# Sigmoid attention and a bilinear feed-forward: x through memory in blocks of 512 tokens, twelve float32 pairs, another spread of the weight decoding

## The chip, the core and the metric

The kernel runs on one core of a Trainium2 chip. The metric is the device time of one execution in microseconds (us); lower is better. Before the change it was 1091.12 us, the median of three runs (1089.79 to 1091.72). One more execution was taken with the hardware profiler on; all views of the profile below are of that execution.

## The reference

```python
# q, k, v: (8 batches, 12 heads, 448 tokens, 64); w1, w2: 768 x 1024; w3: 1024 x 1024; w_out: 1024 x 768
scores = q @ k.T / sqrt(64) - log(448)
attn   = sigmoid(scores) @ v
x      = attn, heads side by side          # 3584 tokens x 768
a, b   = x @ w1, x @ w2
out    = ((a * b) @ w3) @ w_out            # float32
```

The four weights come as float64 (seen as int64 words), so each has to be decoded to float32 on the chip.

## The kernel before, in words

A *pair* is two heads of one batch: 6 pairs in a batch, 48 in all. A pair takes four *slots*, one for each piece of its keys, in the order 0, short (the last 64 keys), 1, 2. A slot puts on TensorE: the scores of the slot, then up to 12 *filler* matmuls, then the attention times v of the slot before (the short piece is held back by one slot more). ScalarE turns scores into sigmoids.

The first `PLAIN` = 9 pairs use float32 matmuls straight on the loaded q, k, v. From then on each operand is split into a high and a low fp32r part, which costs work on VectorE and GpSimd (`split_pair`, `split_v`), two sigmoids for a piece and the subtraction `al` on VectorE. After a pair, `combine` splits its result into `xh` and `xl`, one of the six 128-row pieces (kc) of x for that batch, and keeps it on chip: six tiles of each in `px0` or `px1`, by the parity of the batch.

The filler is `up`: the first products x @ w1 and x @ w2, whose product g is written to memory (`g_dram`). It handles one batch of 448 tokens: 8 chunks of d_ff (fc) times 2 weights times 6 pieces times 3 matmuls, 288 in all, just 12 for each of the 24 slots of a batch. It runs one batch behind attention, so the batch-0 pairs have no filler and the last batch's products come after all attention. A copy of the first accumulator (`a_sb`, ScalarE) and the multiplication (`g`, VectorE) close each fc.

Weights are decoded by "jobs" (`decode_weights`). Jobs 0 to 15 bring w1 and w2, each with one load of 768 KB (`raw`), one ScalarE instruction (`f`), six on VectorE, and then the split into `w` (ScalarE copy, VectorE subtraction). They stand in the first nine pairs, the first eight 3 slots apart, the rest 4/3 slots apart. Jobs 16 to 31 decode w3, half a chunk each, in the second slot of every other pair from pair 12 on, and write it back to memory (`w3_dram`). Each of these loads its raw words right after the job before it has been decoded, two pairs ahead.

After attention: the last batch's `up` beside the decoding of w_out, then w3 @ w_out (w34), then out = g @ w34 in blocks of 512 tokens (`TB`).

The order on TensorE and on SyncE (SP, which issues every DMA) is the order in which the code is written; in the first eight pairs that holds for ScalarE and GpSimd too. VectorE's order, and later ScalarE's and GpSimd's, is chosen by a scheduler at build time. Every engine then works through its list in order, and an instruction that waits holds up all that stand behind it. This holds for SP's DMA issues too.

Of the kernel before, what the change touches and what calls it, by code (L numbers as in the profile page):

```python
# [11 lines left out]
F32 = mybir.dt.float32  # L12
# [13 lines left out]
def sigmoid_attention_bilinear_ffn(  # L26
# [16 lines left out]
    nc = tc.nc  # L43
# [12 lines left out]
    PLAIN = 9  # L56
# [5 lines left out]
    w3_dram = dram.tile([NF, P, NF, P], F32, name="w3_dram")  # L62
    g_dram = dram.tile([NF, P, NT], F32, name="g_dram")

    def split(dst_hi, dst_lo, src, hi_engine, lo_engine):
        hi_engine(out=dst_hi, in_=src)  # L66
        lo_engine.tensor_tensor(out=dst_lo, in0=src, in1=dst_hi, op=ALU.subtract)  # L67

    def load_words(src, pool=None):
        if pool is None:  # L70
            raw = pd.tile([P, NK, P, 2], U32, name="raw", bufs=1)[:, :src.shape[1]]
        else:
            raw = pool.tile([P, *src.shape[1:-1], 2], U32, name="raw")
        nc.sync.dma_start(out=raw, in_=src)
        return raw

    def magnitude(raw):
        f = pd.tile([P, *raw.shape[1:-1]], F32, name="f")
        nc.scalar.activation(f, raw[..., 1].bitcast(F32), AF.Abs, scale=HW_SCALE)  # L79
        return f  # L80
# [26 lines left out]
    px1 = phase_x.enter_context(tc.tile_pool(name="px1", bufs=NK, side="left"))  # L107
    pm = phase_x.enter_context(tc.tile_pool(name="pm", bufs=2, side="left"))
    phase_a = ExitStack()
    px0 = phase_a.enter_context(tc.tile_pool(name="px0", bufs=NK, side="right"))  # L110
    pa = phase_a.enter_context(tc.tile_pool(name="pa", bufs=2, side="right"))
    px = (px0, px1)

    phase_p = ExitStack()
    pp = phase_p.enter_context(tc.tile_pool(name="pp", bufs=3, side="right"))
# [144 lines left out]
    def combine(b, accs):  # L260
        xh = px[b % 2].tile([P, S], F32R, name="xh")
        xl = px[b % 2].tile([P, S], F32R, name="xl")
        if len(accs) == 1:
            split(xh, xl, accs[0][:, :S], nc.scalar.copy, nc.vector)
            return xh, xl
        t = pm.tile([P, S], F32, name="t", bufs=1)
        add_halves(t, [acc[:, :S] for acc in accs])
        split(xh, xl, t, nc.scalar.copy, nc.vector)
        return xh, xl
# [19 lines left out]
    def load_job(i):  # L289
        _, _, cs, src = jobs[i]  # L290
        raws[i] = load_words(src[:, cs], pp) if i < EARLY else load_words(src[:, cs])

    def decode_weights():

        for i, (n, at, cs, _) in enumerate(jobs):
            if i + 2 < EARLY:
                load_job(i + 2)
            for k in (i, i + 1):
                if k not in fs and k in raws:
                    fs[k] = magnitude(raws[k])  # L300
            f = decode(raws.pop(i), fs.pop(i))
            if i + 1 >= EARLY and i + 1 < len(jobs):
                load_job(i + 1)
            if n == 3:
                nc.sync.dma_start(out=w3_dram[at, :, cs], in_=f)
                yield
                continue
            yield
            split(wh[n][:, at, cs], wl[n][:, at, cs], f, nc.scalar.copy, nc.vector)
            yield  # L310

    def up(b, xs, banks):

        for fc in range(NF):
            for n in (1, 2):
                acc = ps.tile([P, 512], F32, name="up", tag=next(banks), bufs=2)
                for kc in range(NK):
                    xh, xl = xs[kc]
                    for m, (w, x) in enumerate(((wh[n], xh), (wh[n], xl), (wl[n], xh))):
                        nc.tensor.matmul(  # L320
                            acc[:, :S], w[:, fc, kc], x,
                            start=(kc == 0 and m == 0), stop=(kc == NK - 1 and m == 2),
                        )
                        if (kc, m) != (NK - 1, 2):
                            yield
                if n == 1:
                    a_sb = pm.tile([P, S], F32, name="a_sb", bufs=1)
                    nc.scalar.copy(out=a_sb, in_=acc[:, :S])
                    yield
            g = pm.tile([P, S], F32, name="g", bufs=1)  # L330
            nc.vector.tensor_tensor(out=g, in0=acc[:, :S], in1=a_sb, op=ALU.mult)
            nc.sync.dma_start(out=g_dram[fc, :, b * S:(b + 1) * S], in_=g)
            yield
# [11 lines left out]
    first = NPAIR * NC  # L345
    starts = [1 + 3 * i for i in range(8)] + [first + 1 + 4 * i // 3 for i in range(8)]
    assert len(starts) == 2 * NF
    later = [(2 * NPAIR + 2 * i) * NC + 1 for i in range(2 * NF)]
    steps = starts + [s + 2 - s // first for s in starts] + later

    EARLY = sum(s < (PLAIN - 1) * NC for s in starts)
# [7 lines left out]
    weights = decode_weights()  # L359
    xs = {b: [] for b in range(B)}  # L360
# [5 lines left out]
    def attend_due(slot):  # L366
        while waiting and waiting[0][0] <= slot:
            _, p, c, ops = waiting.pop(0)
            if c == 0:
                accs[p] = [  # L370
                    ps.tile([P, 512], F32, name="av", bufs=2) for _ in range(1 if p < PLAIN else 2)
                ]
            attend(c, ops, vs[p], accs[p])
            if c == NC - 2:
                b = pairs[p][0]
                xs[b].append(combine(b, accs.pop(p)))
                del vs[p]
# [22 lines left out]
    for p, (b, hp) in enumerate(pairs):  # L400
        if p == PLAIN - 1:
            order.close()
            order.enter_context(tc.manual_schedule(engines={ET.PE, ET.SP}))
        plain = p < PLAIN
        if p == PLAIN - 1:
            phase_p.close()
            pf.append(phase_a.enter_context(tc.tile_pool(name="pf", bufs=2, side="right")))
        qs, kh, kl, ks = splits.pop(p)
        for i, c in enumerate(chunks):
            prepare(p, i)  # L410
# [12 lines left out]
            attend_due(slot)  # L423
            slot += 1
    attend_due(slot)
    take(filler, 10 ** 6)
    take(weights, 10 ** 6)
# [18 lines left out]
    filler = up(B - 1, xs[B - 1], banks)  # L446
# [16 lines left out]
    TB = 512  # L463
# [19 lines left out]
    assert NT % TB == 0  # L483
# [65 lines left out]
```

## Time and profile before

| what | us |
|---|---|
| median of three runs | 1091.12 |
| the profiled execution, whole | 1088.86 |
| its span | 1087.0 |
| TensorE (PE) busy | 1067.2 |
| VectorE (DVE) busy | 720.1 |
| ScalarE (ACT) busy | 563.6 |
| GpSimd (POOL) busy | 194.6 |

In the profile PE is the matmul, PEld the weight load, DVE VectorE, ACT ScalarE, POOL GpSimd, SP or SPq the queue that issues DMAs. L320 is line 320 of the kernel. A row such as `up<-xh,w 128*128 128x448` names the result, the operands and their shapes. "Idle before" names what an engine waited for.

### The profile page before, as it was taken

The numbers are of one execution on the slowest core, as the hardware profiler recorded it, in microseconds if no ns is written. First come the engines' busy times: TensorE is split into PE (matmuls) and PEld (weight loads), VectorE is DVE, ScalarE is ACT, GpSimd is POOL, SyncE is SP. The second block draws the span as 40 slices with busy tenths as digits, with TensorE's granted clock in tenths as the row PEclk, the third lists the DMA queues.
The fourth block names the chain that finished last, engine by engine and source line by source line (L and its number), as shares of the span: only waits on it lengthen the run. The fifth ranks groups of instructions, "written<-read, shape, count | busy, mean of one in ns | idle before, by whom it ended". The sixth has DMA issues, their size and how long they took to land.

```text
span 1087.0 us, 14111 instructions
## 1 busy us (share of the span) xinstructions
PE 1067.2 (98%) x5076; PEld 911.4 (84%) x5076; DVE 720.1 (66%) x1073; ACT 563.6 (52%) x789; POOL 194.6 (18%) x277
## 2 busy tenths in 40 slices
PE   7899899999999999999999999999999999999998
PEld 1246788999999999999999999999999988888886
DVE  6898878888788878887888877749862133123321
ACT  6763567677677776777677766753342011001100
POOL 0002233323323233223323333200000000000000
PEclk9999899999999999999999999999999999999999
DMA  8654444354425336344434534225461032233211
GB/s 265 194 170 126 114 110 130 106 142 124 134 78 161 99 108 162 95 133 116 126 106 128 136 88 106 61 68 183 134 241 51 20 126 77 98 126 126 88 49 48
DMA packets 100693, 129.15 MB, mean 119 GB/s; under 512 B 8016, under 2 KB 82960, under 8 KB 100624
## 3 DMA queue, kind: packets, MB, share of 16 engines
q1 hardware_dynamic: 100624, 128.25, 40.3%
q8 instruction: 40, 0.66, 0.3%
q14 instruction: 29, 0.24, 0.1%
HBM read 98.34 MB, written 29.88 MB: 118 GB/s over the span
## 4 chain that ended last, share of the span: by engine, by line
PE 86%; DVE 9%; DMA 2%; issue 1%; ACT 1%; SPq 1%; DVEq 0%; ACTq 0%
PE up L320 39%; PE up L510 21%; PE av L255 10%; PE sp L199 8%; PE up L494 6%; DVE f L94 1%; PE sp L225 1%; DVE raw L99 1%; DVE w L67 1%; ACT f L79 1%; DVE raw L86 1%; DVE raw L98 1%; DVE f L91 1%; DVE f L102 1%; DVE al L217 0%
## 5 line engine op out<-in xcount | busy, mean ns | idle before, releaser
L320 PE MATMUL up<-xh,w 128*128 128x448 f32 x1536 | 468.2, 368 | 0.0
L320 PEld LDWEIGHTS up<-xh,w 128*128 128x128 f32 x1536 | 289.1, 188 | 32.5 <-issue 6.0
L320 PE MATMUL up<-xl,w 128*128 128x448 f32 x768 | 281.8, 367 | 0.0
L510 PE MATMUL up<-w 128*128 128x512 f32 x1008 | 228.7, 389 | 0.0
L510 PEld LDWEIGHTS up<-w 128*128 128x128 f32 x1008 | 189.2, 188 | 39.3
L180 ACT ACTIVATE ah<-sp,bias 128x896 fp32r<-128x896 f32 x117 | 117.6, 1005 | 110.0 <-PE sp L199 109.4
L67 POOL TENSOR_TENSOR kl<-kk,kh 128x896 fp32r<-128x896 f32 x39 | 87.3, 2238 | 407.6 <-DVE kh L66 407.6
L320 PEld LDWEIGHTS up<-xl,w 128*128 128x128 f32 x768 | 144.6, 188 | 12.9
L217 DVE TENSOR_TENSOR al<-sp,ah 128x896 fp32r<-128x896 f32 x117 | 127.4, 1089 | 42.0 <-ACT sp L180 40.8
L520 DVE COPY o_sb<-up 128x512 f32<-128x512 f32 x42 | 29.0, 691 | 161.0 <-PE up L510 161.0
L66 ACT CAST w<-graw 128x1024 fp32r<-128x1024 f32 x28 | 29.3, 1054 | 175.0 <-PE up L510 170.5
L180 ACT ACTIVATE sp<-sp,bias 128x896 f32<-128x896 f32 x117 | 113.7, 971 | 0.0
L255 PE MATMUL av<-ah,vs 128*128 128x448 f32 x312 | 102.6, 369 | 3.0 <-DVE xl L67 1.4
L67 POOL TENSOR_TENSOR vs<-vv,vs 128x256 fp32r<-128x256 f32 x78 | 71.3, 925 | 100.1 <-DVE vs L66 79.4
L255 PE MATMUL av<-al,vs 128*128 128x448 f32 x234 | 86.3, 369 | 1.5 <-DVE al L217 1.5
L199 PE MATMUL sp<-qs,kh 128*128 128x448 f32 x234 | 86.3, 369 | 0.0
L199 PE MATMUL sp<-qs,kl 128*128 128x448 f32 x234 | 86.2, 369 | 0.0
L239 DVE TENSOR_TENSOR ah<-st,ah 64x448 fp32r<-64x448 f32 x78 | 60.2, 772 | 21.2 <-ACT st L180 19.4
L255 PEld LDWEIGHTS av<-ah,vs 128*128 128x128 f32 x312 | 58.7, 188 | 10.7 <-issue 5.4
L79 ACT ACTIVATE f<-raw 128x768 f32<-128x768 f32 (+2 forms) x48 | 34.1, 710 | 59.9 <-DVE w L67 22.4
L186 ACT COPY t<-av 64x448 f32<-64x448 f32 x78 | 41.2, 529 | 32.4 <-PE av L255 31.3
L180 ACT ACTIVATE ah<-st,bias 64x448 fp32r<-64x448 f32 x78 | 52.2, 669 | 4.1 <-DVE st L187 2.1
(54 smaller groups left out, 1244.7 us busy)
## 6 DMA issues: line engine op xcount, KB each, us to landing
qq<-qT SPq DMA_DIRECT2D x78, 224.0 KB, 3.9
kk<-kT SPq DMA_DIRECT2D x78, 224.0 KB, 4.3
g_dram<-g SPq DMA_DIRECT2D x64, 224.0 KB, 2.0
graw<-g_dram SPq DMA_DIRECT2D x14, 1024.0 KB, 5.3
raw<-w SPq DMA_DIRECT2D x16, 768.0 KB, 5.8
out<-o_sb SPq DMA_DIRECT2D x42, 256.0 KB, 2.0
vv<-vL SPq DMA_DIRECT2D x48, 192.0 KB, 2.7
raw<-w3T SPq DMA_DIRECT2D x16, 512.0 KB, 4.3
```

Source lines behind the costliest of these rows:

```text
L66: hi_engine(out=dst_hi, in_=src)
L67: lo_engine.tensor_tensor(out=dst_lo, in0=src, in1=dst_hi, op=ALU.subtract)
L79: nc.scalar.activation(f, raw[..., 1].bitcast(F32), AF.Abs, scale=HW_SCALE)
L180: nc.scalar.activation(dst, src, AF.Sigmoid, bias=bias[:n], scale=scale)
L186: nc.scalar.copy(out=dst[rows], in_=src[j][others])
L199: nc.tensor.matmul(sp[:, j], k[:, j, at:at + n], qs[:, j], start=m == 0, stop=m == 1)
L217: nc.vector.tensor_tensor(out=al, in0=sp, in1=ah, op=ALU.subtract)
L239: nc.vector.tensor_tensor(out=a[others, j], in0=t[rows], in1=a[rows, j], op=ALU.subtract)
L255: nc.tensor.matmul(accs[j][:, :S], v[:, c, j].rearrange("p u d -> p (u d)"), a[:, j], start=first and m == 0, stop=last and m == len(ops) - 1,
L320: nc.tensor.matmul(acc[:, :S], w[:, fc, kc], x, start=(kc == 0 and m == 0), stop=(kc == NK - 1 and m == 2),)
L494: nc.tensor.matmul(acc[:, :NM], a[:, jc], w[:, jc, ms], start=(jc == 0 and m == 0), stop=(jc == NF - 1 and m == 2),)
L510: nc.tensor.matmul(acc[:, :TB], w[:, fc, ms], g[:, at, fc % NH], start=(fc == 0 and m == 0), stop=(fc == NF - 1 and m == 2),)
```

## The change

1. **x through memory.** After a pair, `combine` now splits into one tile with both parts, and a store (`store_due`) brings it to `x_dram` one slot later (two in the float32 pairs). Only block 0 (tokens 0 to 511: batch 0 and 64 tokens of batch 1) is written straight into its tiles. `load_block` reads blocks 1 to 6 back, 512 KB for each of six pieces. There are eight such tiles: two pieces of the next block are loaded ahead, when fc 6 of the block in work begins; the other four each take the tile of a piece of the block in work, when its last matmul is done.
2. **up in blocks of 512 tokens**, 7 instead of 8, again 288 matmuls each, two batches behind attention: block c starts in the last slot of the first pair of batch c + 2.
3. **PLAIN = 12**: all of batches 0 and 1 is done in float32, without filler beside it.
4. **Jobs 0 to 15** are spread over the first 45 slots, 2.7 slots apart, with the split three slots later; `f` has three buffers instead of two, `raw` four instead of three.
5. **Jobs 16 to 31** stand where they stood, but load their own raw words there: load, decoding and write-back of a job are now written in one slot.

```diff
-    PLAIN = 9
+    TB = 512
+    PLAIN = 2 * NPAIR
+    x_dram = dram.tile([NK, P, 2, NT], F32, name="x_dram")
...
-    def magnitude(raw):
-        f = pd.tile([P, *raw.shape[1:-1]], F32, name="f")
+    def magnitude(raw, pool=pd):
+        f = pool.tile([P, *raw.shape[1:-1]], F32, name="f", bufs=3 if pool is not pd else 2)
...
-    px1 = phase_x.enter_context(tc.tile_pool(name="px1", bufs=NK, side="left"))
+    px = phase_x.enter_context(tc.tile_pool(name="px", bufs=NK + 2, side="left"))
...
-    pp = phase_p.enter_context(tc.tile_pool(name="pp", bufs=3, side="right"))
+    pp = phase_p.enter_context(tc.tile_pool(name="pp", bufs=4, side="right"))
...
+    def combine(b, kc, accs, due):
...
+        at = b * S
+        n = min(max(TB - at, 0), S)
+        if n:
+            if b == 0:
+                blocks[0][kc] = px.tile([P, 2, TB], F32R, name="x")
+            x = blocks[0][kc][:, :, at:at + n]
+            split(x[:, 0], x[:, 1], src[:, :n], nc.scalar.copy, nc.vector)
+        if n < S:
+            x = pa.tile([P, 2, S], F32R, name="xs")[:, :, n:]
+            split(x[:, 0], x[:, 1], src[:, n:], nc.scalar.copy, nc.vector)
+            stores.append((due, x_dram[kc, :, :, at + n:at + S], x))
+
+    def load_block(c, kc):
+        blocks[c][kc] = px.tile([P, 2, TB], F32R, name="x")
+        nc.sync.dma_start(
+            out=blocks[c][kc].bitcast(F32), in_=x_dram[kc, :, :, c * TB:(c + 1) * TB]
+        )
...
-            f = decode(raws.pop(i), fs.pop(i))
-            if i + 1 >= EARLY and i + 1 < len(jobs):
-                load_job(i + 1)
-            if n == 3:
-                nc.sync.dma_start(out=w3_dram[at, :, cs], in_=f)
+    def decode_job(i):
+        if i + 3 < EARLY:
+            load_job(i + 3)
+        elif i >= EARLY:
+            load_job(i)
+        for k in (i, i + 1):
+            if k in raws and k not in fs:
+                fs[k] = magnitude(raws[k], pp if k < EARLY else pd)
+        f = decode(raws.pop(i), fs[i])
+        n, at, cs, _ = jobs[i]
+        if n == 3:
+            nc.sync.dma_start(out=w3_dram[at, :, cs], in_=f)
...
-    def up(b, xs, banks):
+    def up(c, banks):
+
+        xs, following = blocks[c], c + 1 if c + 1 in blocks else None
         for fc in range(NF):
+            if fc == NF - 2 and following:
+                for kc in range(2):
+                    load_block(following, kc)
             for n in (1, 2):
...
+                    if (fc, n) == (NF - 1, 2) and following and kc + 2 < NK:
+                        load_block(following, kc + 2)
...
-    starts = [1 + 3 * i for i in range(8)] + [first + 1 + 4 * i // 3 for i in range(8)]
...
+    EARLY = 2 * NF
+    starts = [1 + 27 * i // 10 for i in range(EARLY)]
+    steps = {s + 3: [(split_job, i)] for i, s in enumerate(starts)}
+    for i, s in enumerate(starts + [(2 * NPAIR + 2 * i) * NC + 1 for i in range(2 * NF)]):
+        steps.setdefault(s, []).append((decode_job, i))
...
+            store_due(slot)
             prepare(p, i)
...
-            take(weights, steps.count(slot))
-            if b > 0 and (hp, i) == (0, 2):
+            for step, n in steps.get(slot, ()):
+                step(n)
+            if b > 1 and (hp, i) == (0, NC - 1):
                 take(filler, 10 ** 6)
-                filler = up(b - 1, xs[b - 1], itertools.repeat("up"))
+                filler = up(b - 2, itertools.repeat("up"))
```

Two places where the order of instructions moves. The first is SP's list around a w3 job. Before the change, for one job in mid-attention (g is the store of a product, vv, qq and kk the inputs of the pairs ahead, `raw<-w3T` the words of a job, `w3_dram<-f` a decoded job written back):

```order
L332 DMA g_dram_67<-g_1925 128x448
L144 DMA vv_1953<-vL 128x3x128
L148 DMA vv_1953<-vL 64x128 x2
L74 DMA raw_1973<-w3T 128x4x256
L305 DMA w3_dram_66<-f_1965 128x512
L135 DMA qq_1995<-qT 64x2x448 x2
L135 DMA kk_1996<-kT 64x2x448 x2
L332 DMA g_dram_67<-g_2059 128x448
```

After the change, for the first pair of batch 3 (pair 18), where block 0 of `up` ends and block 1 begins (`x_dram<-xs` is the store of pair 17's x, `x<-x_dram` the load of a piece of block 1):

```order
L359 DMA g_dram_68<-g_1689 128x512
L286 DMA x_dram_67<-xs_1730 256x1x448
L145 DMA vv_1746<-vL 128x3x128
L149 DMA vv_1746<-vL 64x128 x2
L77 DMA raw_1758<-w3T 128x4x256
L327 DMA w3_dram_66<-f_1760 128x512
L290 DMA x_1781<-x_dram_67 128x2x512
L136 DMA qq_1792<-qT 64x2x448 x2
L136 DMA kk_1793<-kT 64x2x448 x2
L290 DMA x_1814<-x_dram_67 128x2x512
L290 DMA x_1819<-x_dram_67 128x2x512
L290 DMA x_1824<-x_dram_67 128x2x512
```

Before, `raw_1973` belongs to the next job and `f_1965` comes from words that were loaded two pairs earlier; now `f_1760` comes from `raw_1758`, the load just ahead of it in the list, and the last four loads of block 1 stand behind that store. The same rows in the same order stand at pairs 24, 30, 36 and 42: w3 jobs fall on pairs 12, 14, 16, ..., 42, and the blocks change on 18, 24, 30, 36 and 42.

The second is VectorE's list at pair 18 after the change (al of the pair's pieces 1 and 2, the decoding of job 19, then the operands of pair 20 and `al` of pair 19):

```order
L218 TENSOR_TENSOR al_1812<-sp_1798,ah_1809 128x896
L240 TENSOR_TENSOR ah_1803<-st_1753,ah_1803 64x448 x2
L69 CAST vs_1835<-vv_1746 128x4x64 x2
L218 TENSOR_TENSOR al_1848<-sp_1840,ah_1845 128x896
L89 TENSOR_SCALAR raw_1758<-raw_1758 128x512
L94 TENSOR_SCALAR f_1760<-f_1760 128x512
L97 SCALAR_TENSOR_TENSOR f_1760<-f_1760,raw_1758 128x512
L101 TENSOR_SCALAR raw_1758<-f_1760 128x512
L102 SCALAR_TENSOR_TENSOR raw_1758<-raw_1758 128x512
L105 TENSOR_TENSOR f_1760<-f_1760,raw_1758 128x512
L159 CAST qs_1907<-qq_1792 128x896
```

The six instructions of the job now stand together, two slots later than the code names them, between `al` of the fourth slot and the first instruction on the operands of pair 20.

More of the change, by code (lines that the diff above doesn't have):

```diff
@@ L55, in sigmoid_attention_bilinear_ffn @@
     scale = 1.0 / math.sqrt(D)
-    PLAIN = 9
+    TB = 512
+    assert NT % TB == 0 and S <= TB <= 2 * S
+    PLAIN = 2 * NPAIR
     pw = ctx.enter_context(tc.tile_pool(name="pw", bufs=4))
@@ L67, in split, with load_words @@
         lo_engine.tensor_tensor(out=dst_lo, in0=src, in1=dst_hi, op=ALU.subtract)
-    def load_words(src, pool=None):
-        if pool is None:
-            raw = pd.tile([P, NK, P, 2], U32, name="raw", bufs=1)[:, :src.shape[1]]
+    def load_words(src, pool):
+        if pool is pd:
+            raw = pd.tile([P, NF // 2, P, 2], U32, name="raw", bufs=1)
         else:
@@ L258, in attend, with store_due @@
                 )
-    def combine(b, accs):
-        xh = px[b % 2].tile([P, S], F32R, name="xh")
-        xl = px[b % 2].tile([P, S], F32R, name="xl")
+    blocks = {c: {} for c in range(NT // TB)}
+    stores = []
+    def combine(b, kc, accs, due):
         if len(accs) == 1:
[L264 to L269, printed above, removed]
+            src = accs[0][:, :S]
+        else:
+            src = pa.tile([P, S], F32, name="t", bufs=1)
+            add_halves(src, [acc[:, :S] for acc in accs])
+        at = b * S
[9 more added lines that the diff above has]
+            stores.append((due, x_dram[kc, :, :, at + n:at + S], x))
+    def store_due(slot):
+        while stores and stores[0][0] <= slot:
+            _, dst, x = stores.pop(0)
+            nc.sync.dma_start(out=dst, in_=x.bitcast(F32))
+    def load_block(c, kc):
[3 more added lines that the diff above has]
+        )
     wh, wl = {}, {}
@@ L290, in load_job @@
         _, _, cs, src = jobs[i]
[L291 to L300, printed above, removed]
-            f = decode(raws.pop(i), fs.pop(i))
-            if i + 1 >= EARLY and i + 1 < len(jobs):
-                load_job(i + 1)
-            if n == 3:
[L305 to L310, printed above, removed]
@@ L314, in up, with split_job @@
+    def split_job(i):
+        n, at, cs, _ = jobs[i]
+        split(wh[n][:, at, cs], wl[n][:, at, cs], fs.pop(i), nc.scalar.copy, nc.vector)
+    def up(c, banks):
+        xs, following = blocks[c], c + 1 if c + 1 in blocks else None
         for fc in range(NF):
+            if fc == NF - 2 and following:
+                for kc in range(2):
+                    load_block(following, kc)
             for n in (1, 2):
-                acc = ps.tile([P, 512], F32, name="up", tag=next(banks), bufs=2)
+                acc = ps.tile([P, TB], F32, name="up", tag=next(banks), bufs=2)
@@ L325, in up @@
                             yield
+                    if (fc, n) == (NF - 1, 2) and following and kc + 2 < NK:
+                        load_block(following, kc + 2)
                 if n == 1:
-                    a_sb = pm.tile([P, S], F32, name="a_sb", bufs=1)
-                    nc.scalar.copy(out=a_sb, in_=acc[:, :S])
+                    a_sb = pm.tile([P, TB], F32, name="a_sb")
+                    nc.scalar.copy(out=a_sb, in_=acc)
                     yield
-            g = pm.tile([P, S], F32, name="g", bufs=1)
-            nc.vector.tensor_tensor(out=g, in0=acc[:, :S], in1=a_sb, op=ALU.mult)
-            nc.sync.dma_start(out=g_dram[fc, :, b * S:(b + 1) * S], in_=g)
+            g = pm.tile([P, TB], F32, name="g")
+            nc.vector.tensor_tensor(out=g, in0=acc, in1=a_sb, op=ALU.mult)
+            nc.sync.dma_start(out=g_dram[fc, :, c * TB:(c + 1) * TB], in_=g)
             yield
@@ L343, in sigmoid_attention_bilinear_ffn @@
     pairs = [(b, hp) for b in range(B) for hp in range(NPAIR)]
-    first = NPAIR * NC
-    starts = [1 + 3 * i for i in range(8)] + [first + 1 + 4 * i // 3 for i in range(8)]
[L347 to L351, printed above, removed]
+    EARLY = 2 * NF
[3 more added lines that the diff above has]
+        steps.setdefault(s, []).append((decode_job, i))
+    assert len(steps) >= len(starts) and max(starts) + 3 < PLAIN * NC - 2
     qks, vvs = {}, {}
@@ L358, in sigmoid_attention_bilinear_ffn @@
     splits, vs = {0: split_pair(0 < PLAIN, *qks.pop(0))}, {0: split_v(0 < PLAIN, vvs.pop(0))}
-    weights = decode_weights()
-    xs = {b: [] for b in range(B)}
+    load_job(2)
     filler = iter(())
@@ L374, in attend_due @@
             if c == NC - 2:
-                b = pairs[p][0]
-                xs[b].append(combine(b, accs.pop(p)))
+                combine(*pairs[p], accs.pop(p), slot + (2 if p < PLAIN else 1))
                 del vs[p]
@@ L425, in sigmoid_attention_bilinear_ffn @@
     attend_due(slot)
+    store_due(10 ** 6)
     take(filler, 10 ** 6)
-    take(weights, 10 ** 6)
     order.close()
@@ L445, in sigmoid_attention_bilinear_ffn @@
     banks = itertools.cycle(("up", "av"))
-    filler = up(B - 1, xs[B - 1], banks)
+    filler = up(NT // TB - 1, banks)
     for jc in range(NF):
```

24 lines of the change are left out of this document (10 added, 14 removed).

## Prediction, made before the changed kernel was run

> **What bounds the kernel now.** First the busy times, then the windows, to see where TensorE is not full.
>
> ```profile
> PE 1067.2 (98%) x5076; PEld 911.4 (84%) x5076; DVE 720.1 (66%) x1073; ACT 563.6 (52%) x789; POOL 194.6 (18%) x277
> ```
>
> ```profile
> 0.00:26.00 26.00, 20.24 (x72) 5.02 (x72) 15.91 (x24) 15.49 (x18) 0.20 (x4) 1.00 0.86 269
> 52.00:78.00 26.00, 23.89 (x105) 11.34 (x106) 24.07 (x34) 17.81 (x23) 0.00 (x0) 1.00 0.58 175
> 104.00:130.00 26.00, 21.82 (x89) 17.19 (x90) 19.49 (x29) 14.86 (x20) 6.68 (x11) 0.87 0.57 149
> 182.00:208.00 26.00, 26.00 (x129) 23.91 (x129) 21.03 (x33) 19.68 (x29) 9.29 (x14) 1.00 0.54 140
> ```
>
> Behind each window's length stand PE, PEld, DVE, ACT, POOL, then the clock, the DMA share and GB/s. From about 156 us on PE is full. Before that VectorE is: 24.07 of 26 us between 52 and 78. So two stages: a head limited by the decoding on VectorE, and a body limited by matmuls. The chain that ended last gives the body's length:
>
> ```profile
> 156.08 2.46 PE up L320 x12
> ...
> 177.89 1.24 PE av L255 x6
> ...
> 706.08 1.22 PE av L255 x6
> 721.60 2.06 PE av L255 x10
> 723.66 64.43 PE up L320 x312
> 788.09 66.57 PE up L494 x384
> 854.66 228.54 PE up L510 x1008
> ```
>
> The two `av` rows lie 34 pairs apart: 528.2 / 34 = 15.53 us a pair. Twelve fillers take 2.45 us (204 ns each), so 48 take 9.8 and the pair's 28 attention matmuls 5.72. The last matmul ends at 1083.2, 3.8 before the span does.
>
> **The change part by part.** *Width.* The L510 row is the same form at 512 columns: 228.54 / 1008 = 226.7 ns. A pair with filler then takes 5.72 + 48 x 0.2267 = 16.60 us, and 36 pairs have filler: 597.7 us. Block 6 takes 288 x 0.2267 = 65.3, and w34, the output and the end stay at 66.6 + 228.5 + 3.8. From the first scores of pair 12 (I call that T12) on, the kernel thus needs 962 us if PE never waits. In all, 2304 matmuls at 204 ns become 2016 at 226.7: 13 us less. The Trainium skill, TensorE: Matmul & The Clock Gate, section Back-to-back issue gap, gives N / 2.4 + 2.5 ns from one warm matmul to the next; by it (189.2 and 215.8 ns) the width gains under 1 us. The rows differ from it at both widths, and the sum goes by the rows.
>
> *The head.* T12 is set by VectorE. One job of it, undisturbed:
>
> ```profile
> 9.76 0.56 DVE L86 TENSOR_SCALAR raw<-raw 128x768 uint32<-128x768 uint32 x1 [8.90 <-ACT f L79]
> ...
> 32.11 0.56 DVE L86 TENSOR_SCALAR raw<-raw 128x768 uint32<-128x768 uint32 x1 [0.96 <-ACT f L79]
> ...
> 36.64 0.95 DVE L67 TENSOR_TENSOR w<-f,w 128x768 fp32r<-128x768 f32 x1
> 37.51 0.62 DVE L67 TENSOR_TENSOR xl<-av,xh 128x448 fp32r<-128x448 f32 x1
> 38.57 0.56 DVE L86 TENSOR_SCALAR raw<-raw 128x768 uint32<-128x768 uint32 x1 [0.45 <-ACT f L79]
> ```
>
> ```profile
> ACT f L79 <- DVE w L67: 22.4, 12, 4.2
> ```
>
> ```profile
> 13.04 1.02 PE L196 MATMUL sp<-qp 64*128 64x448 f32 x4
> 14.90 1.02 PE L196 MATMUL sp<-qp 64*128 64x448 f32 x4
> ```
>
> Decoding takes 36.64 - 32.11 = 4.53 us, the split 0.87, an x split about 0.6. The waits for `f` come from its two buffers (the 22.4 us), and the third buffer removes them. Jobs now come every 2.7 slots of 1.86 us, 5.0 us, less than the 5.4 + 0.4 that VectorE needs: it stays the limit all through the head. From 9.76: 16 x 4.53 + 14 x 0.87 + 10 x 0.6 ends the last decoding at about 100. ScalarE holds its copy of that job ahead of the last sigmoids, and those, two scores and two `av` take about 5 us more: **T12 = 105**. PE alone would be there at 13 + 45 x 1.86 = 97, which is the lower end; with the stalls of before, 112 the upper. DMA is no limit: at the first window's rate, 269 GB/s at 0.86, the head's 23 MB (16 jobs of 768 KB, twelve pairs of 0.65 MB, the x stores) take about 75 us.
>
> *The step to split operands at pair 12.* Here no filler covers three slots. POOL's kl,
>
> ```profile
> L67 POOL TENSOR_TENSOR kl<-kk,kh 128x896 fp32r<-128x896 f32 x39 | 87.3, 2238 | 407.6 <-DVE kh L66 407.6
> ```
>
> the two sigmoids of 1 us and an `al` of 1.1 stand between the first scores and the first `av`, and the short sigmoid stands on ScalarE behind the `f` of job 16, whose load is only then issued. Before, with filler, the step cost 4 us of idling and then slow matmuls:
>
> ```profile
> 116.31 0.44 PE L255 MATMUL av<-ah,vs 128*128 128x448 f32 x1 [1.33 <-ACT ah L180]
> ...
> 121.20 0.57 PE L199 MATMUL sp<-qs,kh 128*128 128x448 f32 x1
> 121.57 0.57 PE L199 MATMUL sp<-qs,kl 128*128 128x448 f32 x1
> ...
> 126.24 0.36 PE L199 MATMUL sp<-qs,kh 128*128 128x448 f32 x1
> 126.44 0.36 PE L199 MATMUL sp<-qs,kl 128*128 128x448 f32 x1
> ```
>
> Starts are 0.37 us apart after the gap and 0.20 five microseconds later. The Trainium skill, same page, Part 1, says that an idle window of about 3.4 us halves the clock until a busy one of that length; the trace agrees, and by the page each re-warming would cost 1.7 us. I take 6 us for the step (3 to 10).
>
> So far: 105 + 6 + 962 = 1073, against 1087.
>
> *Where the blocks change.* This is what I expect to decide. Before, SP issues a w3 job's write-back straight behind the load of the next job's words, since its own came two pairs earlier:
>
> ```profile
> 416.94 0.38 SPq L144 DMA_DIRECT2D vv<-vL  x1
> 417.37 1.18 SPq L148 DMA_DIRECT2D vv<-vL  x2
> 418.60 0.58 SPq L74 DMA_DIRECT2D raw<-w3T  x1
> 419.23 0.50 SPq L305 DMA_DIRECT2D w_dram<-f  x1
> 419.83 1.31 SPq L135 DMA_DIRECT2D qq<-qT  x2
> 421.19 1.25 SPq L135 DMA_DIRECT2D kk<-kT  x2
> ```
>
> Now that write-back needs the words just requested, and at pairs 18, 24, 30, 36 and 42 the loads of the next block's last four pieces stand behind it. Let T be the start of the second slot (short scores) there. PE runs: short scores and 12 fillers, `av` (T + 3.95), scores and the last 12 fillers (T + 7.49), scores, then the new block's two preloaded pieces, to **T + 9.67**. Then it needs the third piece. SP meanwhile:
>
> ```profile
> 400.50 0.57 PE L225 MATMUL sp<-qs,ks 128*128 128x448 f32 x2
> ```
>
> ```profile
> 403.35 0.61 DVE L67 TENSOR_TENSOR xl<-t,xh 128x448 fp32r<-128x448 f32 x1
> ```
>
> The x split ends 3.5 us after T, and one more VectorE instruction now stands ahead of it: x store at T + 4. Its issue and the three of vv take 2.3, so `raw` is issued at T + 6.3.
>
> ```profile
> raw<-w3T SPq DMA_DIRECT2D x16, 512.0 KB, 4.3
> ...
> w<-w_dram SPq DMA_DIRECT2D x8, 512.0 KB, 4.2
> ```
>
> ```profile
> 423.10 0.69 ACT L79 ACTIVATE f<-raw 128x512 f32<-128x512 f32 x1
> ```
>
> ```profile
> 389.70 0.43 DVE L86 TENSOR_SCALAR raw<-raw 128x512 uint32<-128x512 uint32 x1 [0.61 <-ACT f L79]
> ...
> 391.69 0.69 DVE L99 SCALAR_TENSOR_TENSOR raw<-raw 128x512 f32<-128x512 uint32 x1
> ...
> 398.56 0.69 DVE L102 TENSOR_TENSOR f<-f,raw 128x512 f32<-128x512 f32 x1
> ```
>
> It lands at T + 10.7; `f` 0.7; decoding 2.7 + 0.7 = 3.4: T + 14.9. Write-back 0.6, then the third piece is issued at T + 15.6 and, 512 KB like the w3 loads of 4.2 us, lands at T + 20. Next SP issues qq and kk (2.6 us in the rows above) and only then pieces four to six. The fourth lands at about T + 23.5; PE then does the slot's `av` and the next scores (2 us, twice that at half clock) and starts the fifth between T + 26.3 and T + 28.5 instead of T + 13.1. That is 13 to 15.5 us, and with the clock **15 us a change**, 75 for five (10 to 17 each: 50 to 85). PE has nothing else in its list, so nothing hides it.
>
> After the last pair no job stands in the way, only four loads in a row: the pieces freed from T + 5 on need 2 MB, about 7 us at that same full rate, and come some 2.5 us late.
>
> *The rest.* In the eleven other pairs with a job, qq and kk come at T + 17 and land at T + 24; VectorE and POOL finish at T + 29.5 and pair p + 2 starts at T + 28.9. I take 0 (0 to 1 each, 11). `a_sb` and g grow by a seventh, under a PE slot that grows too: 0. The x traffic adds some 60 GB/s to 140: 0 outside the block changes.
>
> Sum: 1073 + 75 + 2.5 = 1150.5 of span. The profiled execution took 1088.9 for a span of 1087.0 and the median is 2.3 above it, so **1154**.
>
> **The rivals.** (1) *The loads are in time.* If SP reached the third piece by T + 8, or its data were there anyway, the five changes would cost nothing: 1075 + 4 = 1080, faster by 1%. The point from which it decides is (1087 - 1075.5) / 5 = 2.3 us a change. Against it: `raw` alone is issued at T + 6.3 and lands after T + 10. For it: only that in all of the body of before no SP wait reaches PE. 11%. (2) *Only the third piece is late* and the others come with it, 8 to 9 us a change, 42 in all: 1121. For it: DMAs overlap, two of 512 KB come within 5 or 6 us. Against it: qq and kk stand between. 15%. (3) *The other jobs stall too*, 4 us in eleven pairs for late qq and kk: 1198. 6%. (4) *512 columns gain nothing*, the skill's gap rule above taken as what holds in the mixed body: 13 us more than the sum, 1167, inside my range. 3%.
>
> **How the numbers follow.** The forecast (65%) spans 1135 to 1175 by its bounds. The range takes in (2), most of its spread, and (4): 1108 to 1178, leaving out (1), (3) and a little. A measurement tells about 0.2% (2 us) from no change. Faster 0.11, from (1); the same 0.02, the narrow place between (1) and (2); slower 0.87.
>
> **What would show it.** In the profile after: PE should be full from pair 13 on but for five gaps some 100 us apart, each waiting for a DMA `x<-x_dram`; the SP waits should name `f` L105 ahead of L327 at about 9 us a time; the filler rows should show 12 in 2.72 us; T12 should lie at 100 to 110 with no wait of ACT for `w`. The prediction is wrong if PE's gaps at the block changes are under 3 us, if T12 comes after 115, or if other w3 pairs show gaps.

## The result, and the profile after

| | us |
|---|---|
| changed kernel, median of 4 runs | 1184.0 (1182.91 to 1186.92) |
| kernel before, 4 runs beside it | 1091.42 (1089.79 to 1093.82) |
| ratio, 95% interval | 1.0851 [1.0822, 1.0879] |
| span of the profiled execution | 1182.5 (before 1087.0) |

The change makes the kernel 8.5% slower. The forecast was 1154 with a range of 1108 to 1178: right in direction, 30 us short, and 6 us outside the range.

The profile's page for the changed kernel: busy times, then TensorE's busy tenths and its granted clock in 40 slices of 29.6 us.

```profile
PE 1081.8 (91%) x4800; PEld 859.4 (73%) x4800; DVE 682.3 (58%) x1029; ACT 548.9 (46%) x760; POOL 160.3 (14%) x256
...
PE   7887999689968997799779977999999999999998
...
PEclk9989999889998999799979997999999999999999
```

TensorE was full from 156 us on before; now it has five holes, each with a clock below full. Its waits and SP's, over the whole span (total, times, longest), and the landing time of the loads of x:

```profile
PE up L345 <- DMA x<-x_dram: 75.6, 11, 11.5
...
ACT f L82 <- DVE w L70: 4.2, 4, 1.7
```

```profile
SPq L286 <- DVE xs L70: 184.5, 36, 16.1
SPq L327 <- DVE f L105: 145.4, 16, 14.4
```

```profile
x<-x_dram SPq DMA_DIRECT2D x36, 512.0 KB, 6.7
```

All but 0.99 us of the 75.6 fall on the five block changes. One of them in detail, pair 18. TensorE's timeline (start, length, instruction; in brackets the idle time before it and what ended it). The short scores at 216.71 are T; those of the pair before and after are shown too:

```profile
199.94 0.37 PE L226 MATMUL sp<-qs,ks 128*128 128x448 f32 x1
...
216.71 0.57 PE L226 MATMUL sp<-qs,ks 128*128 128x448 f32 x2
...
225.10 1.55 PE L345 MATMUL up<-x,w 128*128 128x512 f32 x6
238.18 1.65 PE L345 MATMUL up<-x,w 128*128 128x512 f32 x3 [11.53 <-DMA x<-x_dram]
...
243.28 1.65 PE L345 MATMUL up<-x,w 128*128 128x512 f32 x3 [3.45 <-DMA x<-x_dram]
...
247.80 1.55 PE L345 MATMUL up<-x,w 128*128 128x512 f32 x6
...
251.39 0.57 PE L226 MATMUL sp<-qs,ks 128*128 128x448 f32 x2
```

A pair without a change takes 216.71 - 199.94 = 16.77 us; this one takes 34.68. So the change of blocks costs 17.9 us here. The other four, read in the same way, cost 18.4, 18.5, 18.6 and 18.7: 92.1 in all. SP's list at that place, and the two instructions that its write-back (L327) waits for, ScalarE's `f` and VectorE's last step of decoding:

```profile
220.02 0.58 SPq L286 DMA_DIRECT2D x_dram<-xs  x1
...
222.76 0.59 SPq L77 DMA_DIRECT2D raw<-w3T  x1
232.62 0.34 SPq L327 DMA_DIRECT2D w_dram<-f  x1
233.06 0.58 SPq L290 DMA_DIRECT2D x<-x_dram  x1
233.73 1.28 SPq L136 DMA_DIRECT2D qq<-qT  x2
235.06 1.25 SPq L136 DMA_DIRECT2D kk<-kT  x2
236.41 1.86 SPq L290 DMA_DIRECT2D x<-x_dram  x3
```

```profile
227.42 0.67 ACT L82 ACTIVATE f<-raw 128x512 f32<-128x512 f32 x1
```

```profile
231.90 0.69 DVE L105 TENSOR_TENSOR f<-f,raw 128x512 f32<-128x512 f32 x1
```

SP issues nothing from 223.35 to 232.62. Windows of the same stretch (length; PE, PEld, DVE, ACT, POOL busy; clock; DMA share; GB/s):

```profile
227.00:233.00 6.00, 0.00 (x0) 0.00 (x0) 5.43 (x10) 1.08 (x2) 1.41 (x2) 0.74 0.00 0
233.00:237.00 4.00, 0.00 (x0) 0.00 (x0) 0.00 (x0) 0.00 (x0) 0.00 (x0) 0.50 0.80 246
237.00:243.00 6.00, 1.65 (x3) 0.83 (x3) 2.34 (x3) 0.00 (x0) 0.23 (x1) 0.50 1.05 281
```

First nothing moves at all while SP stands; then the qq, kk and x loads come together and fill the DMA engines (share 1.05). The clock falls to half while TensorE idles.

The head: the last job's split and the first operands of pair 12, on VectorE, ScalarE, GpSimd and TensorE:

```profile
105.73 0.96 DVE L70 TENSOR_TENSOR w<-f,w 128x768 fp32r<-128x768 f32 x1 [3.98 <-ACT w L69]
...
108.51 2.67 DVE L160 TENSOR_TENSOR qs<-qq,qs 64x896 fp32r<-64x896 f32 x1
```

```profile
103.97 1.01 ACT L181 ACTIVATE ap<-sp,bias 128x896 f32<-128x896 f32 x1 [0.85 <-PE sp L197]
104.88 0.82 ACT L69 CAST w<-f 128x768 fp32r<-128x768 f32 x1
```

```profile
111.32 0.44 PE L200 MATMUL sp<-qs,kh 128*128 128x448 f32 x1 [0.21 <-DVE qs L160]
```

### The profile page after: what moved, and what is told of

Same layout as the page of the kernel before. It is cut to its first block, busy times and chain, and to the rows that moved or that the text cites. A ratio compares the mean times of both kernels' runs of the same rounds, so it can differ in the third digit from the quotient of the medians.

```text
span 1182.5 us, 13620 instructions
## 1 busy us (share of the span) xinstructions
PE 1081.8 (91%) x4800; PEld 859.4 (73%) x4800; DVE 682.3 (58%) x1029; ACT 548.9 (46%) x760; POOL 160.3 (14%) x256
## 4 chain that ended last, share of the span: by engine, by line
PE 84%; DVE 6%; DMA 6%; SPq 2%; issue 1%; ACT 1%; POOL 0%; DVEq 0%; ACTq 0%
PE up L345 38%; PE up L533 19%; PE av L256 9%; PE sp L200 7%; PE up L517 6%; DMA x<-x_dram 3%; PE av L249 2%; PE sp L197 2%; PE sp L226 1%; SPq L136 1%; DVE al L218 1%; DVE f L97 1%; DMA raw<-w 1%; DMA qp<-kT 1%; DVE ah L240 1%
## 5 line engine op out<-in xcount | busy, mean ns | idle before, releaser
L345 PE MATMUL up<-x,w 128*128 128x512 f32 x2016 | 496.0, 396 | 75.6 <-DMA x<-x_dram 75.6
L345 PEld LDWEIGHTS up<-x,w 128*128 128x128 f32 x2016 | 382.8, 191 | 158.8 <-DMA x<-x_dram 82.2
L218 DVE TENSOR_TENSOR al<-sp,ah 128x896 fp32r<-128x896 f32 x108 | 117.6, 1089 | 116.3 <-ACT sp L181 115.8
L70 POOL TENSOR_TENSOR kl<-kk,kh 128x896 fp32r<-128x896 f32 x36 | 76.4, 2121 | 435.9 <-DVE kh L69 308.0
L70 POOL TENSOR_TENSOR vs<-vv,vs 128x256 fp32r<-128x256 f32 x72 | 54.1, 773 | 191.7 <-DVE vs L69 185.0
L249 PE MATMUL av<-ap,vv 128*64 128x448 f32 (+1 forms) x192 | 49.0, 589 | 12.6 <-ACT ap L181 10.6
L240 DVE TENSOR_TENSOR ah<-st,ah 64x448 fp32r<-64x448 f32 x72 | 44.7, 620 | 21.0 <-ACT st L181 19.4
L197 PE MATMUL sp<-qp 64*128 64x448 f32 (+1 forms) x192 | 52.3, 624 | 4.0 <-DMA qp<-kT 4.0
L181 ACT ACTIVATE ap<-sp,bias 128x896 f32<-128x896 f32 (+1 forms) x48 | 47.5, 1002 | 18.1 <-PE sp L197 18.1
L188 DVE TENSOR_TENSOR t<-av,t 64x448 f32<-64x448 f32 x72 | 44.8, 622 | 18.2 <-ACT t L187 16.4
```

The lines of the kernel that those rows point to most:

```text
L181: nc.scalar.activation(dst, src, AF.Sigmoid, bias=bias[:n], scale=scale)
L188: nc.vector.tensor_tensor(out=dst[rows], in0=src[j][rows], in1=dst[rows], op=ALU.add)
L197: nc.tensor.matmul(sp[:, j], kh[rows, at:at + n], qs[rows], start=True, stop=True)
L218: nc.vector.tensor_tensor(out=al, in0=sp, in1=ah, op=ALU.subtract)
L240: nc.vector.tensor_tensor(out=a[others, j], in0=t[rows], in1=a[rows, j], op=ALU.subtract)
L249: nc.tensor.matmul(accs[0][cols, :S], v[:ops[0].shape[0], c, cols], ops[0][:, j], start=first, stop=last,)
```

## The experiments

The theory at the start was the prediction's: the cost is SP, held at the write-back. The rival was that transfers, or something else beside them, set it. "A change" below is the extra time of a pair with a block change over 16.77 us, read from the short scores as above, mean of five; 18.4 in the changed kernel. The first three kernels were run once, the others in several rounds.

| kernel | us | ratio to before [95%] | a change, us |
|---|---|---|---|
| the change | 1184.0 | 1.0851 [1.0822, 1.0879] | 18.4 |
| e1 words ahead | 1172.8 | | 16.0 |
| e2 jobs on odd pairs | 1146.7 | | 11.4 |
| e3 four pieces ahead | 1143.2 | | 10.2 |
| e4 = e1 + e3 | 1114.5 | 1.0243 [1.0211, 1.0276] | 4.1 |
| e5 = e1, store behind | 1126.2 | 1.0318 [1.0288, 1.0348] | 5.8 |
| e6 = e5, fourth piece early | 1133.2 | 1.0394 [1.0379, 1.0410] | 8.5 |
| e7 = e4, store behind | 1119.0 | 1.0254 [1.0232, 1.0277] | 5.2 |
| e8 = e7, copies first | 1117.4 | 1.0255 [1.0232, 1.0277] | 5.0 |
| e9 blocks two slots later | 1134.5 | 1.0397 [1.0376, 1.0418] | 8.3 |
| e10 = e9, copies first | 1133.6 | 1.0391 [1.0369, 1.0413] | 7.9 |
| e11 = e9 + e1 | 1094.2 | 1.0040 [1.0026, 1.0054] | 0.3 |
| e12 = e11 + e3, copies first | 1096.2 | 1.0056 [1.0043, 1.0070] | 0.2 |

**e1, part 5 of the change undone.** The words of a job are requested as soon as the job before it is decoded.

```diff
-        elif i >= EARLY:
-            load_job(i)
...
         f = decode(raws.pop(i), fs[i])
+        if EARLY <= i + 1 < len(jobs):
+            load_job(i + 1)
```

> Theory (the hold): at each block change SP stands about 10 us at a w3 job's write-back, whose words were only requested just before. With the words loaded one job ahead, as in the kernel before, SP should not wait for f any more (145 us in the changed kernel, under 15 here), the third piece should be issued about 8 us after the short scores instead of 16, and each change should cost about 8 us instead of 18: time about 1184 - 50 = 1134. Rival (the transfer): the loads of x, 6.7 us each and with qq and kk between them, set the gap by themselves: then a change still costs over 14 us and the time stays above 1160.

Measured 1172.8: a miss by 39 us, and a time that the rival named (above 1160, over 14 us a change). The wait for `f` at the write-back is gone from SP's list, yet a change still costs 16.0. In e1 T is 216.44. SP's, VectorE's and GpSimd's timelines:

```profile
224.65 0.57 SPq L286 DMA_DIRECT2D x_dram<-xs  x1
...
228.01 0.50 SPq L327 DMA_DIRECT2D w_dram<-f  x1
228.62 0.58 SPq L290 DMA_DIRECT2D x<-x_dram  x1
```

```profile
216.79 0.63 DVE L159 CAST qs<-qq 128x896 fp32r<-128x896 f32 x1 [3.02 <-DMA qq<-qT]
...
220.87 0.63 DVE L69 CAST kh<-kk 128x896 fp32r<-128x896 f32 x1
...
222.07 2.55 DVE L70 TENSOR_TENSOR xs<-t,xs 128x448 fp32r<-128x448 f32 x1
```

```profile
221.63 2.51 POOL L70 TENSOR_TENSOR kl<-kk,kh 128x896 fp32r<-128x896 f32 x1 [8.56 <-DVE kh L69]
```

VectorE at the same place in the changed kernel, where T is 216.71:

```profile
219.37 0.63 DVE L70 TENSOR_TENSOR xs<-t,xs 128x448 fp32r<-128x448 f32 x1
219.91 0.62 DVE L69 CAST kh<-kk 128x896 fp32r<-128x896 f32 x1
```

The write-back now goes out at once (228.01), but SP had stood at the store of x until 224.65, T + 8.2. The changed kernel did not have this hold: there the store goes out at T + 3.3 at all five changes (220.02 at pair 18), in e1 at T + 8.2 to 9.1. In e1 VectorE first waits 3.0 us for qq (3.0 to 4.0 over the five changes), then has `kh` ahead of the split of x (`xs`) and no longer behind it, and takes 2.55 us for `xs` instead of 0.63, beside GpSimd's `kl`. So e1 takes one hold away and brings another: the third piece is issued at T + 12.2 (228.62), only 4.2 us sooner behind T than in the changed kernel (T + 16.4, 233.06).

**e2 and e3.** e2 puts the jobs on the odd pairs, so that none meets a block change. e3 leaves the jobs and gives x ten tiles, so that four pieces are loaded ahead and only two are left for the change (their loads stand ahead of qq and kk).

```diff
-(2 * NPAIR + 2 * i) * NC + 1 for i
+(2 * NPAIR + 2 * i + 1) * NC + 1 for i
```

```diff
-                for kc in range(2):
+                for kc in range(AHEAD):
                     load_block(following, kc)
...
+                        if (fc, n, m) == (NF - 1, 2, 2) and following and kc + AHEAD < NK:
+                            load_block(following, kc + AHEAD)
```

> All w3 jobs one pair later, nothing else: each still loads its words and writes back in one slot, but no job stands where blocks change. Theory (the hold): SP still waits about 9 us for f in 16 places, but none of them is ahead of a piece of x; the third piece is issued 7 us after the short scores, a change costs 6 to 8 us: about 1124. Rival (the transfer): as in the first run, above 1160. A second rival, that the hold also costs something in pairs without a block change (late qq and kk): then gaps appear in the odd pairs and the time lies 10 to 40 us above the first run.

> Ten tiles for x instead of eight, so that four pieces of the next block are loaded ahead, and the last two are issued ahead of qq and kk; the jobs stay as in the changed kernel. Theory (the hold): the fifth piece is still held behind the write-back, issued 16 us after the short scores, landing at 21, needed at 13: 8 to 10 us a change, about 1184 - 45 = 1140. Rival (too few tiles alone): with four pieces ahead nothing waits, about 1094.

e2 came out at 1146.7, 23 us above its expectation, e3 at 1143.2, 3 us above it. In e2 no job stands ahead of the last four pieces, and still TensorE waits (SP's timeline, then TensorE's):

```profile
221.52 0.57 SPq L290 DMA_DIRECT2D x<-x_dram  x1
```

```profile
228.29 1.37 PE L345 MATMUL up<-x,w 128*128 128x512 f32 x3 [4.09 <-DMA x<-x_dram]
233.25 1.65 PE L345 MATMUL up<-x,w 128*128 128x512 f32 x3 [3.59 <-DMA x<-x_dram]
```

The third piece needs 6.8 us from issue to use, not the 4.2 of the prediction, with vv, qq and kk issued around it (DMA share 1.07 from 216 to 221 us, 1.06 from 221 to 224, 1.10 from 224 to 228). The job is not wholly out of the way either: the write-back of pair 17 goes out at 212.89, 1.4 us ahead of the short scores (214.27), and the two pieces loaded ahead, qq and kk come only behind it. In e3, behind the same hold as in the changed kernel, the two pieces that are left go out ahead of qq and kk, and the first of them is in use 4.1 us after its issue (231.99 to 236.11). So transfers that share the engines are a cost beside SP's place.

**e4, e1 and e3 together.**

> Both: words one job ahead and four pieces ahead. Theory: the last two pieces are issued 8 us after the short scores and land at 13 to 14, when they are needed: no gap over 1 us at any block change, about 1184 - 90 = 1094 (1088 to 1100), the time of the kernel before within about 1%. If the transfer or something else of the block changes costs time by itself, it stays above 1105.

1114.5, a miss against 1094 (1088 to 1100): 4.1 us a change are left. What they are was the question of the next four runs.

**e5 to e8.** e5 is e1 with the store of x two slots later, behind vv, the words and three pieces, though ahead of the load that reads it (the last piece of block c + 1 holds the x of the very pair that has just ended). e6 also issues each piece right behind the matmul that frees its tile, so the fourth goes ahead of qq and kk. e7 is e4 with the same late store. e8 adds, in batch 1, ScalarE's two copies ahead of VectorE's two subtractions.

```diff
-                combine(*pairs[p], accs.pop(p), slot + (2 if p < PLAIN else 1))
+                combine(*pairs[p], accs.pop(p), slot + (2 if p < PLAIN else 3))
...
     def load_block(c, kc):
+        if kc == NK - 1:
+            store_due(10 ** 6)
```

```diff
+        if 0 < n < S:
...
+            nc.scalar.copy(out=x[:, 0], in_=src[:, :n])
+            nc.scalar.copy(out=y[:, 0], in_=src[:, n:])
+            for d, part in ((x, src[:, :n]), (y, src[:, n:])):
+                nc.vector.tensor_tensor(out=d[:, 1], in0=part, in1=d[:, 0], op=ALU.subtract)
```

> Edit: e1_words_ahead (the words of a w3 job requested one job ahead) and, added, the store of a pair's x two slots later, though ahead of the load of the last piece of a block. Theory now: two waits stand behind one another on SP ahead of the third piece, the job's write-back (taken away in e1) and the store of the x that VectorE has just split (in e1 SP stood there until 224.65 us, 8.2 us behind the first row of the short scores, and issued the third piece at 228.62). With both gone the third piece is issued when TensorE frees its tile, about 6 us behind the short scores, and lands 5 to 6.7 us later: 2 to 3 us of wait; the fourth stands behind qq and kk and costs about 3 more. A change of blocks then costs about 6 us instead of 16.5 in e1: 1172.8 - 5 x 10.5 = 1120 (1110 to 1130), and SP's wait at the store for VectorE's xs falls from 307 us to below 150. Rival: the loads are slow whenever they are issued (contention with qq, kk and the words), SP's place doesn't matter: within 8 us of e1, 1165 to 1175.

> Edit: e5 with each piece's load issued right behind the matmul that frees its tile, which puts the fourth piece ahead of qq and kk instead of behind them. Theory (SP's order sets the start): the fourth piece starts 2.6 us earlier (four issues of about 0.65 us) and no longer shares the transfers with qq and kk; its part of a change falls from about 3 us to about 0.5, but qq and kk come 0.6 us later: 1107 (1100 to 1114), 12 below e5. Rival (the transfers as a whole set the landing, the order doesn't matter): within 4 us of e5.

> Edit: e4_words_and_pieces_ahead with the store of x placed just ahead of the last piece's load, behind vv, the words, the write-back and the fifth piece. In e4 SP stood at the store until 431.0 us, 5 us behind the short scores, and issued the last two pieces at 434.98; about 4 us a change were left. Theory: the fifth piece goes out when TensorE frees its tile (about 431.5), 3.5 us earlier, and is there in time (needed at 440.5); the sixth goes out at about 432.5. The remaining 4 us a change go: 1114.5 - 5 x 4 = 1094 (1089 to 1098). Rival: what is left in e4 is no wait of the pieces but slow clock and VectorE's chain (qs, al and xs come late once attention bunches up): 1108 to 1115.

> Edit: e7, and in the pairs of the second batch ScalarE's two copies of x's high words stand ahead of VectorE's two subtractions, so that the second copy doesn't wait for the first subtraction (ACT xs L69 <- DVE x L70: 6.5 us in 5 places in the trace of the change). Theory: the six pairs of plain products with decoding are held by that, TensorE's first scores of pair 12 come at 105 to 107 instead of 111.3: 5 below e7, 1089 (1084 to 1094). Rival: the twelve plain pairs are bound by VectorE's decoding as a whole, the order doesn't matter: within 1.5 us of e7.

e5 hit: 1126.2, 47 us below e1, so the store was what held SP in e1. e6 was to be 12 better and is 7 worse; e7 is 4.5 worse than e4 instead of 20 better; e8 gains nothing measurable over e7 although its first scores of pair 12 come at 106.3 instead of 112.8. The chain that ended last shows why e5 to e7 stop there. For e5:

```profile
222.76 7.47 DMA x_dram<-xs
230.28 4.37 DMA x<-x_dram
```

and TensorE behind it, in e5 and then in e6:

```profile
234.69 2.34 PE L347 MATMUL up<-x,w 128*128 128x512 f32 x9 [1.58 <-DMA x<-x_dram]
```

```profile
237.34 4.21 PE L348 MATMUL up<-x,w 128*128 128x512 f32 x9 [4.51 <-DMA x<-x_dram]
```

The last piece's load waits for the store to land, and TensorE waits for that load: 7.5 and 4.4 us in a row, after VectorE (8.5 and 4.3 in e6, 4.8 and 4.4 in e7). Putting the store behind other loads cures SP's hold and lengthens this chain. In e6 the other pieces come earlier, TensorE arrives at the last one earlier (T + 15.8, in e5 T + 17.7) and idles 4.51 us in one go, after which nine matmuls take 4.21 us; in e5 they take 2.34 after 1.58 us of idling. So there is a third cost, a true dependence from pair 17's x to block 1. In the changed kernel it decides nothing: there the store is issued at T + 3.3, and the loads of the last three pieces only from T + 19.7 on.

**e9 and e10.** This dependence can be kept out of the way by starting the blocks two slots later; the first block is spread a little thinner so that no slot stands empty. Everything else is as in the change. e10 adds the copies first.

```diff
-            if b > 1 and (hp, i) == (0, NC - 1):
+            if (b == 2 and (hp, i) == (0, NC - 1)) or (b > 2 and (hp, i) == (1, 1)):
...
-            take(filler, ups)
+            take(filler, ups - (b == 2))
```

> Edit: the changed kernel with one thing moved: a block begins two slots later, in the second slot of an odd pair (the first block is spread thinner, 11 matmuls a slot instead of 12, so that no slot goes without). The words, the write-back, the store of x, the tiles and the lookahead of two pieces stay as in the change. SP then has behind it, when the pieces come free, the store of x, the job and qq and kk; the four pieces stand in a row, and no piece needs an x stored less than a pair before. Theory (a change of blocks costs what SP's order and the path from x's store to its load make of it, not what the pieces themselves are): the third piece comes free 6 to 6.5 us before it is needed and lands in 5 to 6; 0 to 2 us a change with what the clock adds instead of 18.4: 1184 - 5 x 17.4 = 1097 (1091 to 1107). Rival: the transfers are the bound (6.7 us a piece, four in a row sharing with qq and kk), so that the third and the fourth still stall by 3 to 4 us together, and with half clock behind it 6 to 8 us a change: 1125 to 1135.

> Edit: e9 with ScalarE's two copies ahead of VectorE's two subtractions in the second batch (as in e8, where the first scores of pair 12 came 6.5 us earlier than in e7 but its short scores, which wait for the split of kk, only 3.5). Theory: 2 to 4 us below e9, 1094 (1088 to 1104). Rival: nothing of it comes through: within 1 us of e9.

e9 gave 1134.5: the number that the rival named, though not for its reason. SP's timeline and TensorE's:

```profile
231.18 0.34 SPq L327 DMA_DIRECT2D w_dram<-f  x1
...
234.80 2.52 SPq L290 DMA_DIRECT2D x<-x_dram  x4
```

```profile
239.86 3.02 PE L345 MATMUL up<-x,w 128*128 128x512 f32 x6 [8.03 <-DMA x<-x_dram]
```

I had written that SP would have the job behind it by then. It had not: the write-back still held it until 231.18, and the pieces were issued 3 us after TensorE had stopped (239.86 - 8.03 = 231.83). e10 is within 1 us of e9, as its rival said.

**e11 and e12.** e11 takes both holds' causes away: blocks two slots later, and the words one job ahead. Eight tiles and two pieces ahead, as in the change. e12 has all the edits, except the store's.

> Edit: e9 and e1 together, a block begins two slots later and the words of a w3 job are requested one job ahead; tiles and lookahead as in the change. In e9 the write-back still held SP until 231.18 us, 17.6 behind the short scores of the pair before, and the four pieces were issued only at 234.80, 3.0 us behind the point at which TensorE stood still (239.86 - 8.03 = 231.83); they then came in 5.1 us. Here nothing holds SP when the third piece comes free, some 6 us ahead of its use, and no piece needs a fresh store. Theory (SP's order makes the cost; the transfers themselves fit): 8.2 us a change in e9 become 0 to 1.5: 1134.5 - 5 x 7.5 = 1097 (1091 to 1105). Rival (transfers: 2 MB in a row behind qq and kk with the 16 engines over 90% busy at up to 395 GB/s, as e9's trace shows): the third piece still stalls by 3 us and the clock adds 1, 1115 to 1120.

> Edit: e11 with four pieces ahead (ten tiles, as in e3) and ScalarE's copies first (as in e8). Theory: no wait for x at all, 16.8 us in every pair; from the change's span 1182.5 without its five block changes (92.0 above six pairs each) and without 2 to 3 us at pair 12: 1088 of span, 1090 (1086 to 1096), no measurable difference from before, so that 512 columns with memory in between win nothing here that the head and the slower filler matmuls (229 ns in the mix) don't take back. Rival (something else holds the changes, VectorE's chain at the job pairs or the clock): 1100 to 1115.

e11 hit: 1094.2, with 0.3 us a change. Of the waits for x, the matmuls have one of 0.3 us left and the weight loads three short ones:

```profile
PEld up L345 <- DMA x<-x_dram: 1.6, 3, 0.7
```

SP's timeline of e11, the window in which the four pieces come, and TensorE's timeline:

```profile
221.78 4.18 SPq L290 DMA_DIRECT2D x<-x_dram  x4
```

```profile
222.00:230.00 8.00, 8.00 (x38) 6.83 (x37) 7.83 (x12) 4.36 (x7) 0.00 (x0) 1.00 1.07 316
```

```profile
227.86 2.91 PE L345 MATMUL up<-x,w 128*128 128x512 f32 x12
```

The same 2 MB behind the same qq and kk fill the DMA engines as before (share 1.07), but TensorE is busy for all 8.00 us. Block 1 begins with the row at 227.86 and needs its third piece in the middle of it, some 7.5 us after the first of the four issues; in the changed kernel the first issue came when TensorE stood still already. The hold that e1 brought is not there: the two pieces loaded ahead now go out behind qq and kk (207.00 against 203.41 for qq), VectorE waits for qq at most 0.3 us, and the store of x goes out at T + 2.9 to 3.0 at all five changes. e12, 1096.2, misses its range (1086 to 1096) by 0.2 us: with no waits for x left to save, two more tiles and earlier copies bring nothing. No kernel here beats the one before; e11, the best, is 0.4% slower.

## Why the prediction was right and wrong

*Right, and shown by runs:* the mechanism and its places. Five gaps about 119 us apart, each waiting for x, at pairs 18, 24, 30, 36 and 42; taking the hold away and starting the blocks later (e11) returned 1184.0 - 1094.2 = 89.8 of the 92.1 us. Rivals (1) and (2), that the loads come in time or only one is late, are refuted by the changed kernel's trace (two gaps a change, 11.5 and 3.5 us), and (3), that other jobs' pairs stall too, by their length: from pair 13 on every pair without a change takes 16.77 or 16.78 us, with a job or without.

*Right in detail:* the steps up to the write-back. In T + ..., predicted and measured: `raw` issued 6.3 and 6.1, `f` 10.7 and 10.7, decoded 14.9 and 15.9, third piece issued 15.6 and 16.4. The waits of `f` for a buffer went from 22.4 to 4.2 us, and none of the other pairs with a job from pair 14 on cost anything.

*The step that failed, the largest of the terms that were too small:* "The fourth lands at about T + 23.5", and with it **15 us a change**. A change took 18.4. The third piece was there at T + 21.5 instead of 20, the fourth at T + 26.6 (243.28, issued within the row at 236.41), and the fifth began at T + 31.1 instead of 26.3 to 28.5. The prediction priced the loads by a w3 load's row, 4.2 us, and let qq and kk cost SP only their issue. Of the 3.1 us by which the fourth was late, 0.9 lie in its issue (T + 19.7, where the forecast's steps give 18.8) and 2.2 in its load, 6.9 us instead of 4.7. The windows show what was left out: SP's hold bunches 0.9 MB of qq and kk and 2 MB of x into one stretch that fills the DMA engines (246 and 281 GB/s at shares of 0.80 and 1.05), so that each load takes longer, and the clock is at half. In e3, with two pieces ahead of qq and kk behind the same hold, the first took 4.1 us; no run takes qq and kk away, so their part in it is not measured by itself. 5 x 3.4 = 17 us.

*Also too small, in "so far 1073":* three smaller terms. T12 came at 111.3, not 105. The last decoding ended at 100.8 as predicted, but the 5 us after it were 10.5: ScalarE's copy of the last `w`, put ahead of the sigmoids in the forecast, stands behind one at 104.88, then VectorE splits it, and then come the pair's operands with one instruction slowed to 2.67 us: +6.3. A pair takes 16.77 us, not 16.60 (12 fillers take 2.75 between other matmuls, not 2.72, which is 0.12 of the 0.17): +6 over 36 pairs. The step at pair 12 took 8.6 and not 6: 17.1 us from the first scores to the end of the third slot's attention, with 8.5 us of matmuls in them. The last change cost 0.99 and not 2.5. With the blocks' 17 these make 30 of the 32 us between 1150.5 and 1182.5. Without the blocks' 17 us, or without the other terms' 15, the time would have lain inside the range.

Rival (4), no gain from 512 columns, concerns the filler matmuls alone. The chain that ended last of the changed kernel has them as

```profile
129.43 2.75 PE up L345 x12
```

which makes 2016 x 2.75 / 12 = 462 us, against 2304 x 2.46 / 12 = 472 before: a gain of 10 us, near the 13 of the rows, and not the less than 1 that the Trainium skill's gap rule (TensorE: Matmul & The Clock Gate, section Back-to-back issue gap), cited in the prediction, gives.

The same terms answer the question of what the 512 columns are worth. Without its block changes the changed kernel would have a span of 1182.5 - 92.1 = 1090.4, and e11 has 1091.0; the forecast for that case (rival 1) was 1075. The forecast's gain ahead of the block changes, 1087 - 1073 = 14 us, was taken by the three terms above, in the head, the step at pair 12 and the pairs' rate. Of the head, only the order of ScalarE's copies of x was tried: in e8, e10 and e12 the first scores of pair 12 come at 106 to 108, but the short scores behind them, which need the split of kk, at best 3.5 us sooner, and nothing of it can be told in the time. Nothing else was tried there.

*Wrong in my reading of the first experiments:* I took the write-back for the only thing in the way, and after e1 the store of x for a hold that had lain behind it. The traces say otherwise. In the changed kernel the store goes out on time, at T + 3.3; it is late in e1, where VectorE's order differs and qq comes late. The way of a fresh x through memory (7.5 and 4.4 us in e5) counts where the store is put behind other loads. So the 18.4 us of the changed kernel are the write-back and the loads that meet behind it, and the other two costs are what single edits ran into. e1's edit alone gives back 2.4 us a change, e9's alone 10.1, and both together 18.1. Why VectorE's order moved with e1's edit stays open.

## What to carry to other kernels

A queue that issues in order hands the lateness of its slowest producer to every load written behind it, and when it is released they all meet at the DMA engines: price such a hold with the transfers landing together, not one by one. Taking one such wait away can bring another, as in e1, so list all waits that stand ahead of the late load again after each edit, and judge the pair of edits, not each by itself. Where data goes out to memory and comes back, leave the store's and the load's landing, here 9 to 13 us (e5 to e7), between the producer and the first use.

## What the runs showed of the hardware beyond that

VectorE's subtraction of two operands that both lie in SBUF is slowed while GpSimd works on `kl`: in e1 ten of the rows `xs<-t,xs` begin within a `kl` and take 2.54 to 2.55 us, the 26 others 0.61 to 0.65. In the changed kernel six begin in the last 0.15 to 0.44 us of a `kl` and take 0.64 to 0.93. Rows that take one operand from a matmul accumulator (`al`, `st`) keep their 1.09 and 0.62 us beside it. The Trainium skill, GPSIMD Engine Reference, section Key points, says that GpSimd shares its SBUF interfaces with VectorE, with contention for VectorE's instructions that have two SBUF inputs; these rows agree. In e1 this is 1.9 of the 4.9 us by which the store at pair 18 comes later behind T.

What TensorE loses beyond an idle stretch itself can't be told from the length of that stretch alone. In e6 nine filler matmuls took 4.21 us at all five changes, after waits of 4.3 to 4.7 us, and in e5 2.33 to 2.35 us, after waits of 1.5 to 3.0. But in e4 they took 3.68 to 3.92 us in three of the five changes, after waits of only 1.4 to 1.7 us, and 2.33 and 2.34 in the other two. The first of them:

```profile
233.96 3.90 PE L353 MATMUL up<-x,w 128*128 128x512 f32 x9 [1.67 <-DMA x<-x_dram]
```

Its clock was 0.58 between 234 and 238 us; in e5 it was 1.00 between the same times, with the row at 234.69.
